# Two quads side by side through h's products on four PSUM banks, conversions doubled in other tiles of the first phase, the last product's three sums in tiles apart

## The chip, the core and the metric

One core of one Trainium2 chip. The metric is the device time of one execution in microseconds; the figures given are medians of several runs. The engines are PE (TensorE), DVE (VectorE), ACT (ScalarE), POOL (GpSimd) and SP, whose queue issues the transfers (DMA).

## What is computed

Three layers in a row on 4608 tokens, all in float32: attention within chunks of 64 tokens, then two feed-forward layers. The change is mostly in the last one, and a little in how the weights of the last two are converted.

```python
def _moe_ref(x, w_in, w_out, g_ln):          # 512 -> 1024 -> 512
    h = x @ w_in
    e = np.exp(h - np.max(h, axis=-1, keepdims=True))
    solu = h * (e / (np.sum(e, axis=-1, keepdims=True) + 1e-09))
    ...
    ln = (solu - mu) / np.sqrt(var + 1e-06) * g_ln
    return ln @ w_out

def _moe2_ref(x, w_in, w_out):               # 512 -> 2048 -> 512
    h = x @ w_in
    g = np.maximum(0.01 * h, h)
    return g @ w_out
```

The weights arrive as 64-bit words and are turned into float32 on the chip.

## The kernel before, in words

**First phase, 36 tiles of 128 tokens.** Loop t does attention, the first feed-forward layer and, beside them, the conversion of the weights of the last layer. A tile's order on PE is: half of ff1's products, transposes (pt), then for most tiles a block of 24 y matmuls (L499), then the x product (L389), which needs ACT's copy pt (L379), which stands behind the reduction z on DVE (L432) and the exponential on ACT (L434). In every fourth tile from t = 5 on (`late`: 5, 9, 13, ...) the y matmuls come at the tile's end, so they don't stand ahead of the x product. 40 pieces of weights are converted: normally one per tile, two in the tiles that the table `DOUBLE` names. A conversion is four instructions on DVE (L108, L110, L114, L118) and one on ACT. Every second piece completes a pair, and the pair step follows (`want_blocks`: DVE L191 and L192, five copies and subtractions on ACT and POOL) at the end of its tile.

**Last layer, six groups of 768 tokens.** Both products are done by seven products of half-size blocks instead of eight (the names p1 to p7, in the order `PRODUCTS`: p1, p6, p2, p7, p5, p4, p3). A float32 operand is split into a high and a low part (`operand`: ACT copies the high part, DVE subtracts it for the low one, L270 and L271), and each product is three matmuls: high by high, high by low, low by high.

*h's products* (the h stage, `h2_product`, L824): a quad is two blocks of 128 columns of the hidden layer, 8 quads per group. A quad has seven products of six matmuls of 384 columns; each product has weights of its own (`w_s`, a ring of 9 tiles, a load of 256 KB for each in the order of use, `w_order`). The products lie in three chains, each in one PSUM bank: p1 and p2 add up; p6, p7 and p4 add up; p5 and p3 add up. Between them a reader takes what is there so far: ACT copies p1 and takes p2 through the leaky function; DVE adds p1 to p6 (u2) and to p7 (u3), u3 to p5, p1 to p4, u2 to p3 (all L835), and ACT takes the last three through the leaky function (L806). There are two banks, `ptx` and `s`, and even and odd quads take them in opposite order. Two quads make a pair. After p5 of the odd quad the pair's first block is split for the next stage (`block_split`), in the next pair's first quad three sums of blocks are made on DVE (`block_sum`, L865).

*Output products* (`out_product`, `out_matmuls`, L883 and L901): 28 slots of 12 matmuls, seven products by four pairs. The sums of three tiles of 128 tokens lie in one PSUM tile of three banks, `o0` for the products 0, 2, 4, 6 and `o1` for 1, 3, 5, and `result` takes them out in adds over all three banks (L923). In the last group the last product is done one tile of tokens after the other, so that its results can leave in turn (L893 for the third).

Within each engine the order is the program's; an instruction behind a waiting one waits too.

## Time and profile before

| | |
|---|---|
| median of 3 runs (lowest to highest) | 1313.31 us (1312.67 to 1314.63) |
| profiled execution / its span | 1316.21 us / 1314.4 us |
| PE / weight loads / DVE / ACT / POOL busy | 96% / 84% / 67% / 43% / 21% of the span |
| mean granted clock of PE | 0.994 |
| first phase | up to 563.05 us |
| second group: h's products / output products | 687.17 to 752.03 / 752.03 to 811.37 us |
| a group, from start to start | 124.2 us |

PE is busy nearly all the time, so the time is to be looked for in what PE waits for and in the spacing of its matmuls; busy time of PE counts matmuls that overlap in its pipeline, and a matmul that is shown with 339 ns may follow the one ahead by half of that.

### The profile page before, as it was taken

The numbers are of one execution on the slowest core, as the hardware profiler recorded it, in microseconds if no ns is written. First come the engines' busy times: TensorE is split into PE (matmuls) and PEld (weight loads), VectorE is DVE, ScalarE is ACT, GpSimd is POOL, SyncE is SP. The second block draws the span as 40 slices with busy tenths as digits, with TensorE's granted clock in tenths as the row PEclk, the third lists the DMA queues.
The fourth block names the chain that finished last, engine by engine and source line by source line (L and its number), as shares of the span: only waits on it lengthen the run. The fifth ranks groups of instructions, "written<-read, shape, count | busy, mean of one in ns | idle before, by whom it ended". The sixth has DMA issues, their size and how long they took to land.

```text
span 1314.4 us, 21334 instructions
## 1 busy us (share of the span) xinstructions
PE 1259.7 (96%) x7978; PEld 1104.6 (84%) x7978; DVE 879.8 (67%) x1280; ACT 567.9 (43%) x1006; POOL 270.5 (21%) x356
## 2 busy tenths in 40 slices
PE   6999999999999999999999999999999999999998
PEld 4778887887888788898888989888889898889887
DVE  8777776777677675435784677567656765774574
ACT  6655444544554454423433352343334323443350
POOL 0346554564555464100000000000000000000000
PEclk9999999999999999999999999999999999999999
DMA  8534555666566564278888778878987898788575
GB/s 241 152 103 136 191 174 169 209 225 181 167 192 207 154 201 131 100 252 262 276 282 294 237 244 293 270 241 259 293 268 227 258 294 257 237 269 271 169 218 182
DMA packets 171638, 288.73 MB, mean 220 GB/s; under 512 B 50576, under 2 KB 81296, under 8 KB 170512
## 3 DMA queue, kind: packets, MB, share of 16 engines
q1 hardware_dynamic: 171152, 286.78, 69.6%
q8 instruction: 64, 1.05, 0.3%
q10 hardware_dynamic: 384, 0.59, 0.2%
q14 instruction: 38, 0.31, 0.1%
HBM read 239.08 MB, written 48.23 MB: 219 GB/s over the span
## 4 chain that ended last, share of the span: by engine, by line
PE 84%; DVE 6%; ACT 4%; issue 2%; POOL 1%; DMA 1%; ACTq 0%; SPq 0%; DVEq 0%; POOLq 0%
PE h_ps L824 25%; PE o_ps L883 18%; PE y_ps L499 13%; PE h_ps L417 11%; PE o_ps L901 9%; PE x_ps L389 3%; PE s_ps L340 2%; PE ln_ps L472 2%; DVE h_c L835 2%; DMA kbd<-in_k 1%; ACT yo L270 1%; PE pt_ps L373 1%; DVE lnT L487 1%; ACT c L806 1%; DVE es L353 1%
## 5 line engine op out<-in xcount | busy, mean ns | idle before, releaser
L824 PE MATMUL h_ps<-yo,w_s 128*128 128x384 f32 x2016 | 366.3, 339 | 23.9 <-DVE h_c L835 23.8
L824 PEld LDWEIGHTS h_ps<-yo,w_s 128*128 128x128 f32 x2016 | 349.5, 188 | 39.9 <-DVE h_c L835 35.8
L883 PE MATMUL o_ps<-wo_s,yo 128*128 128x512 f32 x1000 | 353.5, 397 | 0.0
L901 PE MATMUL o_ps<-wo_s,yo 128*128 128x256 f32 x1008 | 283.7, 281 | 0.0
L883 PEld LDWEIGHTS o_ps<-wo_s,yo 128*128 128x128 f32 x1000 | 187.7, 188 | 46.2
L417 PE MATMUL h_ps<-wi,xs 128*128 128x512 f32 x864 | 210.7, 397 | 2.6 <-ACT xs L403 1.4
L499 PE MATMUL y_ps<-lnT,wo 128*128 128x512 f32 (+1 forms) x888 | 205.2, 387 | 1.7 <-DVE lnT L487 0.9
L417 PEld LDWEIGHTS h_ps<-wi,xs 128*128 128x128 f32 x864 | 159.8, 189 | 38.3 <-ACT xs L403 2.7
L499 PEld LDWEIGHTS y_ps<-lnT,wo 128*128 128x128 f32 x888 | 161.4, 188 | 35.4 <-DVE lnT L487 2.0
L901 PEld LDWEIGHTS o_ps<-wo_s,yo 128*128 128x128 f32 x1008 | 190.0, 188 | 0.0
L271 DVE TENSOR_TENSOR yo<-c,yo 128x768 fp32r<-128x768 f32 x144 | 132.5, 952 | 31.9 <-ACT yo L270 31.9
L806 ACT ACTIVATE c<-h_c 128x384 f32<-128x384 f32 x144 | 74.2, 525 | 176.7 <-DVE h_c L835 174.7
L835 DVE TENSOR_TENSOR h_u<-h_ps,h_p 128x384 f32<-128x384 f32 x96 | 53.4, 556 | 124.6 <-PE h_ps L824 124.6
L270 ACT ACTIVATE yo<-c 128x768 fp32r<-128x768 f32 x144 | 113.1, 839 | 8.4 <-DVE c L865 6.8
L439 DVE SCALAR_TENSOR_TENSOR us<-h_ps,us 128x1024 f32<-128x1024 f32 x36 | 44.1, 1224 | 58.8 <-ACT us L434 58.8
L835 DVE TENSOR_TENSOR h_c<-h_ps,h_u 128x384 f32<-128x384 f32 x96 | 53.2, 554 | 33.4 <-PE h_ps L824 30.1
L487 DVE TENSOR_TENSOR lnT<-ln_ps,lnT 128x512 fp32r<-128x512 f32 x72 | 46.1, 683 | 33.6 <-ACT lnT L483 33.5
L363 POOL TENSOR_TENSOR es<-es,st 128x512 f32<-128x512 f32 x33 | 34.6, 1049 | 160.6 <-DVE st L362 151.1
L270 ACT ACTIVATE yo<-a 128x768 fp32r<-128x768 f32 x36 | 30.0, 842 | 72.8 <-DVE a L265 72.8
L389 PEld LDWEIGHTS x_ps<-pt,vbd 128*64 128x64 f32 x1152 | 39.1, 145 | 22.2 <-ACT pt L379 12.4
L507 ACT ACTIVATE ys<-y_ps 128x512 f32<-128x512 f32 x36 | 21.5, 597 | 83.1 <-PE y_ps L499 81.9
L806 ACT ACTIVATE c<-h_ps 128x384 f32<-128x384 f32 x48 | 23.6, 493 | 76.3 <-PE h_ps L824 76.3
(91 smaller groups left out, 1429.3 us busy)
## 6 DMA issues: line engine op xcount, KB each, us to landing
w_s<-wi_d SPq DMA_DIRECT2D x336, 256.0 KB, 3.4
wo_s<-wo_d SPq DMA_DIRECT2D x168, 512.0 KB, 4.5
wi_d<-wi SPq DMA_DIRECT2D x8, 1792.0 KB, 6.5
wo_d<-wi SPq DMA_DIRECT2D x8, 1792.0 KB, 6.8
raw<-in_w_out SPq DMA_DIRECT2D x24, 512.0 KB, 5.2
raw<-in_w_in SPq DMA_DIRECT2D x23, 512.0 KB, 5.3
vbd<-in_v SPq DMA_DIRECT2D x72, 128.0 KB, 4.6
a<-y_d SPq DMA_DIRECT2D x24, 384.0 KB, 4.4
```

The source lines that it names most:

```text
L270: act.activation(o[:, 0], x, AF.Copy)
L271: dve.tensor_tensor(o[:, 1], x, o[:, 0].bitcast(F32), op=ALU.subtract)
L389: pe.matmul(ps[e * D : (e + 1) * D, i, c * D : (c + 1) * D], lhsT=vv[:, i, c, e], rhs=pp[:, i, c * D : (c + 1) * D], start=True, stop=True,)
L417: pe.matmul(h[:, n, :], lhsT=x[:, a, kk, :], rhs=w[:, b, kk % 2, n, :], start=(kk == 0 and a == 0 and b == 0), stop=(kk == KD - 1 and a == 1),
L439: dve.scalar_tensor_tensor(u, h, 1.0 / FF1, u, op0=ALU.mult, op1=ALU.mult, accum_out=z[:, 2:3])
L487: dve.tensor_tensor(dst[:, 1], ps, dst[:, 0].bitcast(F32), op=ALU.subtract)
L499: pe.matmul(ps[:, part], lhsT=w[:, a, kk % 4, m * P : (m + 1) * P], rhs=lnT[:, c, kk, pairs, :][:, part], start=(kk == 0 and a == 0 and c ...
L806: act.activation(blocks[block, j // 2][:, j % 2], src, AF.Prelu, alpha=0.01)
L824: pe.matmul(ps, lhsT=w[:, a, kk * P : (kk + 1) * P], rhs=y[:, c, kk, :], start=(first and kk == 0 and a == 0 and c == 0), stop=(kk == 1 an ...
L835: dve.tensor_tensor(o, ps, x, op=ALU.add)
L883: pe.matmul(ps, lhsT=x[:, 0, kk, c], rhs=w[:, kk].rearrange("p a n -> p (a n)"), start=first, stop=False, skip_group_check=True,)
L901: pe.matmul(ps[:, : 2 * P], lhsT=x[:, 1, kk, c], rhs=w[:, kk, 0], start=False, stop=last, skip_group_check=True,)
```

## The change

Three edits.

1. The h stage takes two quads at a time: each product is done for both quads of a pair before the next product. The second quad's chains lie in two further banks, `b0` and `b1`. These are taken from the output sums: `o1` is now three tiles `b0`, `b1`, `b2` of a bank each, so its adds are done per bank. Loads, sums and splits are put at the corresponding places of the new order.
2. `DOUBLE` names other tiles: 10, 18 and 26 are out, 15, 23 and 31 are in.
3. In the last group the sums of the last product are three tiles of their own (`ptx`, `s`, and the third bank of `o`), and each result is taken out right behind its matmuls.

```diff
@@ -41,7 +41,7 @@
 RING = 11
 
 AHEAD = 5
-DOUBLE = (5, 6, 7, 10, 14, 18, 22, 26, 30)
+DOUBLE = (5, 6, 7, 14, 15, 22, 23, 30, 31)
 
 LN_SCALE = float(FF1) ** -3
 
@@ -277,7 +277,13 @@
             yo[g, PRODUCTS[k]] = operand(x)
 
     w_tiles = []
-    w_order = ((j, name) for _ in range(NG) for j in range(QUADS) for name in PRODUCTS)
+    w_order = (
+        (2 * u + i, name)
+        for _ in range(NG)
+        for u in range(PAIRS)
+        for name in PRODUCTS
+        for i in range(2)
+    )
 
     def w_load():
         at = next(w_order, None)
@@ -810,12 +816,15 @@
         def h2_product(n, k):
             g, j = divmod(n, QUADS)
             name = PRODUCTS[k]
-            even = n % 2 == 0
-            if k < 2:
-                banks[n, k] = bank(("ptx", "s")[k if even else 1 - k], "h2_ps")[:, :TH]
-            ps = banks[n, 0 if name in ("p1", "p2", "p5", "p3") else 1]
-            if k == 4:
-                ps = banks[n, 0] = bank(("ptx", "s")[0 if even else 1], "h2_ps")[:, :TH]
+            i, even = n % 2, n // 2 % 2 == 0
+            chain = 0 if name in ("p1", "p2", "p5", "p3") else 1
+            if name in ("p1", "p6", "p5"):
+                at = chain if even else 1 - chain
+                if i == 0:
+                    banks[n, chain] = bank(("ptx", "s")[at], "h2_ps")[:, :TH]
+                else:
+                    banks[n, chain] = pso.tile([P, 512], F32, tag=f"b{at}", name="h2_ps")[:, :TH]
+            ps = banks[n, chain]
             w, y = w_tiles.pop(0), yo[g, name]
             w_load()
             first, last = name in ("p1", "p6", "p5"), name in ("p2", "p4", "p3")
@@ -836,20 +845,20 @@
                 return o
 
             if name == "p1":
-                p = kept["p1"] = wb.tile([P, TH], F32, tag="h_p1", bufs=2, name="h_p1")
+                p = kept["p1", i] = wb.tile([P, TH], F32, tag="h_p1", bufs=2, name="h_p1")
                 act.activation(p, ps, AF.Copy)
             elif name == "p6":
-                kept["u2"] = with_ps("u2", kept["p1"])
+                kept["u2", i] = with_ps("u2", kept["p1", i])
             elif name == "p2":
                 leaky(n, "c11", ps)
             elif name == "p7":
-                kept["u3"] = with_ps("u3", kept["p1"])
+                kept["u3", i] = with_ps("u3", kept["p1", i])
             elif name == "p5":
-                leaky(n, "c22", with_ps("c", kept["u3"]))
+                leaky(n, "c22", with_ps("c", kept["u3", i]))
             elif name == "p4":
-                leaky(n, "c21", with_ps("c", kept["p1"]))
+                leaky(n, "c21", with_ps("c", kept["p1", i]))
             else:
-                leaky(n, "c12", with_ps("c", kept["u2"]))
+                leaky(n, "c12", with_ps("c", kept["u2", i]))
 
         def block_sum(name, i):
             x, y, op, to = {
@@ -875,7 +884,7 @@
 
         def out_matmuls(p, i, kk, m, whole=True):
             x, w = operands[p * PAIRS + i], wo_now[i]
-            ps = sums[p % 2][:, m]
+            ps = sums[p % 2][m]
             first = p in (0, 1, 4) and i == 0 and kk == 0
             last = i == PAIRS - 1 and kk == 1
             c = slice(m * P, (m + 1) * P)
@@ -909,10 +918,21 @@
 
         wo_now, results = {}, {}
 
-        def out_product(s):
+        def out_banks(p, apart):
+
+            if p == 1:
+                sums[1] = [pso.tile([P, 512], F32, tag=f"b{m}", name="o_ps") for m in range(3)]
+            else:
+                o = pso.tile([P, 3, 512], F32, tag="o", name="o_ps")
+                sums[0] = [o[:, m] for m in range(3)]
+                if apart:
+                    sums[0][:2] = [bank(tag, "o_ps") for tag in ("ptx", "s")]
+                sums["whole"] = None if apart else o
+
+        def out_product(s, apart):
             p, i = divmod(s, PAIRS)
             if i == 0 and p in (0, 1, 4):
-                sums[p % 2] = pso.tile([P, 3, 512], F32, tag=f"o{p % 2}", name="o_ps")
+                out_banks(p, apart and p == 4)
             wo_now[i] = wo_tiles.pop(0)
             wo_load()
             for kk in range(2):
@@ -920,7 +940,12 @@
                     out_matmuls(p, i, kk, m)
 
         def plus(o, p, a, x, m=slice(0, 3)):
-            dve.tensor_tensor(o[:, m], sums[p % 2][:, m, a * 2 * P : (a + 1) * 2 * P], x[:, m], op=ALU.add)
+            c = slice(a * 2 * P, (a + 1) * 2 * P)
+            if p % 2 == 0 and sums["whole"] is not None:
+                dve.tensor_tensor(o[:, m], sums["whole"][:, m, c], x[:, m], op=ALU.add)
+                return
+            for i in range(m.start, m.stop):
+                dve.tensor_tensor(o[:, i], sums[p % 2][i][:, c], x[:, i], op=ALU.add)
 
         def result(p, m=slice(0, 3), halves=(1, 0)):
 
@@ -940,7 +965,7 @@
             o = results[to]
             for a in halves:
                 if x is None:
-                    act.activation(o[:, m], sums[p % 2][:, m, 2 * P :], AF.Copy)
+                    act.activation(o[:, m], sums["whole"][:, m, 2 * P :], AF.Copy)
                 else:
                     plus(o, p, a, results[x], m)
                 x = to
@@ -957,28 +982,30 @@
             )
 
         for g in range(NG):
-            for j in range(QUADS):
-                if g == 0 and j < WOS:
-                    wo_load()
-                elif g and j == 1:
-                    out_store(g - 1, 6)
-                elif g and 2 <= j < 6:
-                    y_load(g + 1, j - 2)
-                for k in range(7):
-                    h2_product(g * QUADS + j, k)
-                    if g and j == 7 and k < 2:
-                        y_sum(g + 1, ("s1", "s3")[k])
-                    if j % 2 == 1 and k == 4:
-                        block_split(j // 2)
-                    if j % 2 == 0 and j and 1 <= k < 4:
-                        block_sum(("s1", "s3", "s2")[k - 1], j // 2 - 1)
+            for u in range(PAIRS):
+                for m in range(14):
+                    if m in (0, 7):
+                        if g == 0 and u < 3:
+                            wo_load()
+                        elif g and (u, m) == (0, 7):
+                            out_store(g - 1, 6)
+                        elif g and u in (1, 2):
+                            y_load(g + 1, 2 * u - 2 + m // 7)
+                    k, i = divmod(m, 2)
+                    h2_product(g * QUADS + 2 * u + i, k)
+                    if g and u == 3 and m in (0, 7):
+                        y_sum(g + 1, "s3" if m else "s1")
+                    if m == 8:
+                        block_split(u)
+                    if u and m in (2, 4, 6):
+                        block_sum(("s1", "s3", "s2")[m // 2 - 1], u - 1)
             for s in range(SLOTS):
                 p, i = divmod(s, PAIRS)
                 tail = g == NG - 1 and p == 6
                 if tail:
                     wo_now[i] = wo_tiles.pop(0)
                 else:
-                    out_product(s)
+                    out_product(s, g == NG - 1)
                 if s < 2:
                     for name in ("s1", "s3") if s == 0 else ("s2",):
                         block_sum(name, PAIRS - 1)
@@ -1007,9 +1034,9 @@
             for i in range(PAIRS):
                 for kk in range(2):
                     out_matmuls(6, i, kk, m, whole=m < 2)
-            if m:
-                result(6, slice(m - 1, m))
-                out_store(NG - 1, 6, sync, slice(m - 1, m))
+            if m < 2:
+                result(6, slice(m, m + 1))
+                out_store(NG - 1, 6, sync, slice(m, m + 1))
         result(6, slice(2, 3), (0,))
         for eng, rows in ((sync, slice(0, 64)), (act, slice(64, P))):
             out_store(NG - 1, 6, eng, slice(2, 3), rows)
```

On PE, at the end of the first pair and the start of the second (h2_ps are the banks' tiles, yo the operands in the order of the products, w_s the weights), before:

```order
L824 MATMUL h2_ps_5789<-yo_5510,w_s_5689 128x384 x6
L824 MATMUL h2_ps_5759<-yo_5513,w_s_5699 128x384 x6
L824 MATMUL h2_ps_5789<-yo_5516,w_s_5710 128x384 x6
L824 MATMUL h2_ps_5828<-yo_5493,w_s_5722 128x384 x6
L824 MATMUL h2_ps_5839<-yo_5500,w_s_5734 128x384 x6
L824 MATMUL h2_ps_5828<-yo_5504,w_s_5749 128x384 x6
```

and after:

```order
L833 MATMUL h2_ps_5752<-yo_5510,w_s_5392 128x384 x6
L833 MATMUL h2_ps_5768<-yo_5510,w_s_5668 128x384 x6
L833 MATMUL h2_ps_5689<-yo_5513,w_s_5679 128x384 x6
L833 MATMUL h2_ps_5700<-yo_5513,w_s_5690 128x384 x6
L833 MATMUL h2_ps_5752<-yo_5516,w_s_5701 128x384 x6
L833 MATMUL h2_ps_5768<-yo_5516,w_s_5711 128x384 x6
L833 MATMUL h2_ps_5828<-yo_5493,w_s_5721 128x384 x6
L833 MATMUL h2_ps_5839<-yo_5493,w_s_5730 128x384 x6
```

Before, these are p5, p4, p3 of the odd quad and p1, p6, p2 of the next one, each on the bank of the product two ahead; now each operand stands twice in a row and a bank comes back after four products.

DVE at the same place (h_u2, h_u3 and h_c are the adds, the yo row is the second half of the block's split, s1 a sum of blocks), before:

```order
L835 TENSOR_TENSOR h_u3_5787<-h2_ps_5759,h_p1_5757 128x384
L835 TENSOR_TENSOR h_c_5798<-h2_ps_5789,h_u3_5787 128x384
L271 TENSOR_TENSOR yo_5801<-c110_5697,yo_5801 128x768
L835 TENSOR_TENSOR h_c_5812<-h2_ps_5759,h_p1_5757 128x384
L835 TENSOR_TENSOR h_c_5823<-h2_ps_5789,h_u2_5768 128x384
L835 TENSOR_TENSOR h_u2_5848<-h2_ps_5839,h_p1_5837 128x384
L865 TENSOR_TENSOR s10_5850<-c210_5732,c220_5720 128x768
```

and after:

```order
L844 TENSOR_TENSOR h_u3_5750<-h2_ps_5700,h_p1_5687 128x384
L844 TENSOR_TENSOR h_c_5761<-h2_ps_5752,h_u3_5738 128x384
L271 TENSOR_TENSOR yo_5765<-c110_5719,yo_5765 128x768
L844 TENSOR_TENSOR h_c_5777<-h2_ps_5768,h_u3_5750 128x384
L844 TENSOR_TENSOR h_c_5788<-h2_ps_5689,h_p1_5676 128x384
L844 TENSOR_TENSOR h_c_5800<-h2_ps_5700,h_p1_5687 128x384
L844 TENSOR_TENSOR h_c_5811<-h2_ps_5752,h_u2_5698 128x384
L844 TENSOR_TENSOR h_c_5823<-h2_ps_5768,h_u2_5709 128x384
L844 TENSOR_TENSOR h_u2_5859<-h2_ps_5850,h_p1_5837 128x384
L874 TENSOR_TENSOR s10_5861<-c210_5790,c220_5763 128x768
```

The split stood between the odd quad's adds of p5 and p4; now it stands between the p5 adds of the first and the second quad, with five adds behind it until the next pair.

DVE in the first phase, from the end of t = 12 to the start of t = 13, before:

```order
L353 TENSOR_TENSOR es_2054<-s_ps_2036,st8_2052 128x512
L487 TENSOR_TENSOR lnT_449<-ln_ps_2057,lnT_449 128x4x128
L487 TENSOR_TENSOR lnT_449<-ln_ps_2062,lnT_449 128x4x128
L191 TENSOR_TENSOR wc_2083<-wf_1949,wc_2083 128x256
L192 TENSOR_TENSOR wc_2083<-wf_1809,wc_2083 128x256
L432 TENSOR_REDUCE z_2098<-h_ps_1951 128x1
L439 SCALAR_TENSOR_TENSOR us_2100,z_2098<-h_ps_1951,us_2100 128x1024
```

and after:

```order
L359 TENSOR_TENSOR es_2046<-s_ps_2028,st8_2044 128x512
L493 TENSOR_TENSOR lnT_449<-ln_ps_2049,lnT_449 128x4x128
L493 TENSOR_TENSOR lnT_449<-ln_ps_2054,lnT_449 128x4x128
L438 TENSOR_REDUCE z_2077<-h_ps_1943 128x1
L445 SCALAR_TENSOR_TENSOR us_2079,z_2077<-h_ps_1943,us_2079 128x1024
```

The pair step (the two wc rows) stood ahead of the reduction z of t = 13; now it is at the end of t = 11 and of t = 13.

DVE at t = 15, between the softmax's reciprocal and x's split, before:

```order
L362 RECIPROCAL st8_2503<-st8_2503 128x8
L108 TENSOR_SCALAR wf_2553<-wf_2553 128x512
L110 TENSOR_SCALAR wf_2553<-wf_2553 128x512
L114 SCALAR_TENSOR_TENSOR wf_2553<-raw_2131,wf_2553 128x512
L118 SCALAR_TENSOR_TENSOR wf_2553<-raw_2131,wf_2553 128x512
L407 TENSOR_TENSOR xs_2652<-x_ps_2622,xs_2652 128x512
```

and after:

```order
L368 RECIPROCAL st8_2343<-st8_2343 128x8
L108 TENSOR_SCALAR wf_2393<-wf_2393 128x512
L108 TENSOR_SCALAR wf_2395<-wf_2395 128x512
L110 TENSOR_SCALAR wf_2393<-wf_2393 128x512
L110 TENSOR_SCALAR wf_2395<-wf_2395 128x512
L114 SCALAR_TENSOR_TENSOR wf_2393<-raw_1970,wf_2393 128x512
L114 SCALAR_TENSOR_TENSOR wf_2395<-raw_2110,wf_2395 128x512
L118 SCALAR_TENSOR_TENSOR wf_2393<-raw_1970,wf_2393 128x512
L118 SCALAR_TENSOR_TENSOR wf_2395<-raw_2110,wf_2395 128x512
L413 TENSOR_TENSOR xs_2500<-x_ps_2470,xs_2500 128x512
```

One conversion, now two; the same holds for t = 23 and 31, and t = 10, 18 and 26 have one instead of two.

PE in the last product of the last group, from the second to the third tile of tokens (with the engines that a row waits for), before:

```order
L901 MATMUL o_ps_12449<-wo_s_12538,yo_12582 128x256
L883 MATMUL o_ps_12449<-wo_s_12538,yo_12582 128x512
L901 MATMUL o_ps_12449<-wo_s_12538,yo_12582 128x256
L893 MATMUL o_ps_12449<-wo_s_12484,yo_12535 128x256 [waits DVE_49]
L893 MATMUL o_ps_12449<-wo_s_12484,yo_12535 128x256
L901 MATMUL o_ps_12449<-wo_s_12484,yo_12535 128x256
```

and after:

```order
L910 MATMUL o_ps_12531<-wo_s_12624,yo_12668 128x256
L892 MATMUL o_ps_12531<-wo_s_12624,yo_12668 128x512
L910 MATMUL o_ps_12531<-wo_s_12624,yo_12668 128x256
L902 MATMUL o_ps_12529<-wo_s_12566,yo_12621 128x256 x2
L910 MATMUL o_ps_12529<-wo_s_12566,yo_12621 128x256
L902 MATMUL o_ps_12529<-wo_s_12566,yo_12621 128x256 x2
```

The third part wrote into the same tile as the second and waited for DVE; now it has a tile of its own and no wait at that place.

## Rows read from the trace of the kernel before

**Rows 1.** The page, costliest groups: busy us, mean ns | idle before, releaser

```profile
L824 PE MATMUL h_ps<-yo,w_s 128*128 128x384 f32 x2016 | 366.3, 339 | 23.9 <-DVE h_c L835 23.8
```

**Rows 2.** Timeline of PE, 683 to 760: start, us, what [idle before <-releaser]

```profile
687.17 14.83 PE L824 MATMUL h_ps<-yo,w_s 128*128 128x384 f32 x84
703.32 15.43 PE L824 MATMUL h_ps<-yo,w_s 128*128 128x384 f32 x84 [1.32 <-DVE h_c L835]
...
752.03 0.39 PE L883 MATMUL o_ps<-wo_s,yo 128*128 128x512 f32 x1
```

**Rows 3.** The chain of waits in order of time, 686 to 722: start, us, what

```profile
687.33 12.59 PE h_ps L824 x72
```

**Rows 4.** Timeline of all engines, 700 to 722, end of an odd quad

```profile
716.70 0.56 DVE L835 TENSOR_TENSOR h_c<-h_ps,h_u 128x384 f32<-128x384 f32 x1 [0.48 <-PE h_ps L824]
...
718.58 0.96 DVE L271 TENSOR_TENSOR yo<-c,yo 128x768 fp32r<-128x768 f32 x1 [1.33 <-ACT yo L270]
...
719.46 0.55 DVE L835 TENSOR_TENSOR h_c<-h_ps,h_p 128x384 f32<-128x384 f32 x1
```

**Rows 5.** Windows: length, busy PE, PEld, DVE, ACT, POOL (count), PEclk, DMA, GB/s

```profile
201.50:203.20 1.70, 1.70 (x19) 1.37 (x15) 1.63 (x3) 0.72 (x3) 1.53 (x4) 0.50 0.97 405
564.00:574.00 10.00, 10.00 (x59) 10.00 (x58) 3.35 (x6) 3.24 (x7) 0.00 (x0) 1.00 0.87 283
687.00:703.00 16.00, 15.00 (x86) 14.63 (x85) 7.54 (x12) 4.69 (x9) 0.00 (x0) 1.00 0.94 314
703.00:712.00 9.00, 8.68 (x47) 8.15 (x48) 5.97 (x10) 3.03 (x6) 0.00 (x0) 1.00 0.81 252
752.00:811.50 59.50, 59.50 (x339) 51.70 (x338) 46.38 (x53) 25.78 (x35) 0.00 (x0) 1.00 0.82 257
```

**Rows 6.** DMA over one h stage, 687.17 to 752.03

```profile
DMA packets 9839, 17.34 MB, mean 267 GB/s; under 512 B 979, under 2 KB 2771, under 8 KB 9835
```

**Rows 7.** Timeline of PE, first phase, tiles 9, 13 and 17

```profile
138.18 0.60 PE L373 MATMUL pt_ps<-ident,es 128*128 128x128 f32 x4
...
152.80 0.60 PE L373 MATMUL pt_ps<-ident,es 128*128 128x128 f32 x4
...
195.96 0.60 PE L373 MATMUL pt_ps<-ident,es 128*128 128x128 f32 x4
...
199.67 1.89 PE L389 MATMUL x_ps<-pt,vbd 128*64 128x64 f32 x32 [2.24 <-ACT pt L379]
...
214.28 0.60 PE L373 MATMUL pt_ps<-ident,es 128*128 128x128 f32 x4
...
258.89 1.15 PE L389 MATMUL x_ps<-pt,vbd 128*64 128x64 f32 x32
```

**Rows 8.** Timeline of DVE and ACT there: z, a double, a single conversion, pt

```profile
196.11 1.21 DVE L432 TENSOR_REDUCE z<-h_ps 128x1 f32<-128x1024 f32 x1
...
215.64 1.59 DVE L108 TENSOR_SCALAR wf<-wf 128x512 f32<-128x512 f32 x2
...
219.03 1.28 DVE L118 SCALAR_TENSOR_TENSOR wf<-raw,wf 128x512 uint32<-128x512 uint32 x2
...
233.48 0.38 DVE L108 TENSOR_SCALAR wf<-wf 128x512 f32<-128x512 f32 x1
...
236.52 0.69 DVE L407 TENSOR_TENSOR xs<-x_ps,xs 128x512 fp32r<-128x512 f32 x1
...
255.32 1.21 DVE L432 TENSOR_REDUCE z<-h_ps 128x1 f32<-128x1024 f32 x1
...
258.24 0.59 ACT L379 ACTIVATE pt<-pt_ps 128x512 f32<-128x512 f32 x1
```

**Rows 9.** Timeline of the last 9 us

```profile
1305.77 0.88 DVE L923 TENSOR_TENSOR o_u<-o_ps,o_u 128x256 f32<-128x256 f32 x2 [3.70 <-PE o_ps L901]
...
1306.70 0.50 PE L893 MATMUL o_ps<-wo_s,yo 128*128 128x256 f32 x2 [0.98 <-DVE o_u L923]
...
1309.84 1.22 DVE L923 TENSOR_TENSOR o_u<-o_ps,o_u 128x256 f32<-128x256 f32 x3 [3.19 <-PE o_ps L901]
```

## The prediction, as it was made before the result

> **What bounds the kernel now.** I read the page first: the group of h's products, L824, is the only one of PE's large groups with idle time ahead of it, 23.9 us, nearly all put down to one add of DVE, h_c [rows 1]. So I looked at PE alone in one of the six groups of 768 tokens. The stretch of h's products (the h stage) runs from 687.17 to 752.03, 64.86 us, in four runs of 84 matmuls with a hole of 1.32 us ahead of each but the first [rows 2]; the other five groups show the same four runs and the same three holes. What would it take with no wait? The chain of waits gives it: at a group's start 72 matmuls follow one another in 12.59 us with nothing between them, 174.9 ns each or 1.049 us per product of six [rows 3]. 336 of them make 58.77 us. The h stage is therefore 6.09 us over its own pace: 3 x 1.32 = 3.96 us in the holes and 2.1 us in waits too short to show as holes.
>
> Why the hole? At the end of the odd quad DVE does p5's add at 716.70. Then comes the split's second half (yo), which waits 1.33 us for ACT, and only behind it p4's add, over at 719.46 + 0.55 = 720.01 [rows 4]. That add frees the bank in which the next quad begins. From p5's add to a free bank are 3.31 us. PE has two products to do meanwhile, 2 x 1.049 less the 0.16 us by which a matmul's 339 ns stick out over the pace [rows 1, 3], 1.93 us. The difference, 1.38 us, is the hole of 1.32 within 0.06, so this arithmetic can be used for the change.
>
> Is 174.9 ns a floor? In 564 to 574 the weight loads are busy 10.00 of 10.00 us at full clock [rows 5]: matmul behind matmul, each with weights of its own. And can the weights come faster? The stage moved 17.34 MB [rows 6]; at the 314 GB/s of its first 16 us [rows 5] that takes 55.2 us, less than 58.77.
>
> **The change, part by part.**
>
> *Two quads side by side.* The number of matmuls and adds stays. Between a product and the next use of its bank there are now three others instead of one. The tightest place is p3 of the second quad: it needs p5's add of that quad, which stands behind the split on DVE, in the place where p4's add stood. From the end of the first quad's p5, PE does p5, p4, p4, p3: 4 x 1.049 - 0.16 = 4.03 us, against 3.31 + 0.05 for the add. 0.67 us are left. The next pair's first products take the banks of p4 and p3, whose adds follow on DVE at 0.55 us each [rows 4] or as soon as their product is done, and which PE wants only one by one, 1.05 us apart. The sums that now stand between u2's and u3's adds are followed by three products. In the last pair of four groups an extra sum goes ahead of p5's add; it eats the 0.67 us at most about once per group, which I take as nothing. The first group's second product takes a bank that the first phase's last copies read: once, and one product's 1.05 us at most; also nothing. Taken: all 6.09 us go, 6 x 6.09 = 36.5 us. Ends: 6 x 3.96 = 23.8 us if only the holes go, 36.5 us.
>
> *Order of the weight loads, sums and stores.* The same number of equal loads in the order of use; the store and the loads of y on SP's queue stay ahead of the same products (7, 14, 21, 28, 35), and the block's split stands behind the first quad's p5, three products after the p2 that completes the block. Nothing.
>
> *Conversions doubled in other tiles.* In the first phase every fourth tile (t = 5, 9, 13, ...) is one in which PE has no y matmuls ahead of the x product. At t = 13, 21 and 29 PE waits there for ACT's copy pt, 2.24 us at 199.67 [rows 7]. DVE's pair step (L191, L192) of the tile before stood ahead of the reduction z, which began at 196.11, only after the tile's transposes of 195.96. The x product begins 3.56 us after z there, and 3.57 us at t = 17 (258.89 after 255.32), where no pair step stood ahead and PE didn't wait [rows 7, 8]: z sets it. The tile t = 13 takes 214.28 - 195.96 = 18.32 us, t = 9 takes 152.80 - 138.18 = 14.62 [rows 7]: 3.70 us, of which 1.46 are PE at half clock after the hole (0.50 at 201.5 [rows 5]). In the new table no late tile has a pair step ahead: 3 x 3.70 = 11.1 us gained.
>
> But t = 14 and 15 are both doubled (so are 22, 23 and 30, 31). A single conversion keeps DVE from 233.48 to 236.52, 3.04 us, and is over exactly when x's split is ready; a double one takes from 215.64 to 219.03 + 1.28 = 220.31, 4.67 us [rows 8]. t = 14 has slack, as a tile after a late one. t = 15 has none, since DVE enters it just as late as it now enters with a single one. So DVE leaves t = 15 1.63 us later, and t = 16 has no idle time in which to win that back. At t = 16 PE's y matmuls still cover it; at t = 17 nothing does: the copy pt, at 258.24 + 0.59 only 0.06 us ahead of the x product at 258.89 [rows 7, 8], comes 1.57 us too late. New holes of 1.57 us at t = 17, 25 and 33: 4.7 us. Does the clock fall after them? After 1.32 us it doesn't (1.00 in 703 to 712, right behind such a hole), after 2.24 it does [rows 5, 7]; 1.57 is nearer the former, so I take no fall. With a fall it is 3 x 1.46 = 4.4 us more. Net gain 11.1 - 4.7 = 6.4 us; ends 2.0 and 11.1.
>
> *Adds in three parts.* The second sum now lies in three tiles, so three sums per group are added in 18 adds of 256 instead of 6 of 768. An add of 256 takes 0.44 us [rows 9], all 18 take 7.9 us. Even as pure addition, DVE would be busy 46.38 + 7.9 = 54.3 of the 59.5 us of an output stage, in which PE is busy throughout [rows 5]; each sum has at least four slots of products before its banks are wanted. Nothing. A rule speaks against it: by the Trainium skill ("VectorE: DVE Perf Modes", section "The TRN2 errata") an instruction pays a fixed extra, once for a large tile and each time for many small ones. The trace agrees: 384 elements take 0.55 us and 256 take 0.44 [rows 4, 9], so some 0.2 us don't depend on the size. If those of the 12 further adds per group lay on the path, 6 x 12 x 0.2 = 14 us, the sum below would be 30 us instead of 45; they lie under PE's products.
>
> *The tail.* Now the sums of the last product share a tile: PE waits 0.98 us for the add of part two before it may write part three, and the last add is the third of three that follow 1309.84 (1.22 us) [rows 9]. With tiles apart PE ends 0.98 us sooner and one add of 0.44 is left of 1.22: 0.98 + 0.78 = 1.8 us. Ends 0.8 and 2.0.
>
> **The sum.** 36.5 + 6.4 + 1.8 = 44.7 us. The profiled execution took 1316.2 us (span 1314.4): 1271.5. The median of the runs is 2.9 us lower, so 1313.3 - 44.7 = 1268.6 us.
>
> **Rivals.**
> - *The clock falls after the new holes* too: 1268.6 + 4.4 = 1273.0. The hole lies between the two lengths seen. 0.22.
> - *No new holes*, because DVE finds the 1.63 us somewhere: 1263.9. Against it: no idle row of DVE in t = 15 and 16 but those in which it waits for ACT in its own chain. 0.15.
> - *DMA sets the h stage.* A faster PE asks for more at once. If 283 GB/s (564 to 574) is what the weights get at best, the stage takes 17.34 MB / 283 = 61.3 us and gives only 3.6 us per group: 1283.7. Against: 314 GB/s in [rows 5]. 0.08.
> - *The holes move instead of going.* If DVE's chain for two quads is 1.32 us longer than I make it, p3 of each pair waits 0.65 us, 24 x 0.65 = 15.6 us: 1284.2. 0.06.
> - *Slower:* the 252 GB/s of 703 to 712, where y loads run beside the weights, are a ceiling and not merely what was asked for. Then the h stage takes 17.34 / 252 = 68.8 us, 3.9 longer than now, and 6 x 3.9 - 6.4 - 1.8 gives 1328.7. It decides below 262 GB/s (66.2 us, which uses up the other gains). Against: a DMA share of 0.81 there and 0.94 in 687 to 703. 0.03, and 0.01 for landing on no change.
> - *A lower floor:* if the 174.9 ns still hold waits too short to see, and PE streams a column per cycle of its 2.4 GHz (a granted clock of 1.00), 384 columns take 160 ns, and 14.9 ns x 2016 = 30 us more go: 1238.6. Against: the stretch without waits has weight loads busy throughout [rows 3, 5]. 0.03. The Trainium skill ("TensorE: Matmul & The Clock Gate", section "Back-to-back issue gap") gives columns / 2.4 + 2.5 ns, 162.5 ns here, by which the sum would be 25 us larger; this trace is 12.4 ns above it.
>
> **How the numbers follow.** The forecast has the rest, 0.42. With the two cases beside it, 1263.9 to 1273.0 hold 0.79; unknown small waits in the h stage and the two cases at 1284 pull the upper end: 1262 to 1284. Within 0.2% (2.6 us, about what a measurement of this kernel tells from no change) 0.01, slower 0.04, faster 0.95.
>
> **What would show it.** After: h stages of 58.8 us without holes at L833 (61 would speak for DMA, with waits for w_s loads; holes at p3 with h_c as releaser for DVE); no hole before x at t = 13, 21, 29 and holes of about 1.6 us at t = 17, 25, 33, with a granted clock of 1.00 or 0.50 behind them; no wait ahead of L902 and the last add alone. Wrong would be above all an h stage that keeps its 64.9 us.

## The result and the profile after

| | before | after |
|---|---|---|
| median (lowest to highest) | 1313.38 us (1312.67 to 1314.63) | 1266.2 us (1265.91 to 1266.87) |
| profiled execution / its span | 1316.21 / 1314.4 us | 1266.87 / 1265.1 us |
| PE / weight loads / DVE / ACT busy | 96 / 84 / 67 / 43% | 98 / 87 / 69 / 45% |
| first matmul of h's products | 563.05 us | 555.29 us |
| h stage of the second group | 64.86 us | 58.35 us |

The ratio is 0.9641, 95% interval 0.9624 to 0.9657: 47.2 us less, where 44.7 were forecast (1268.6 us, range 1262 to 1284).

The costliest groups on the page of the kernel after, with the DMA issues for h's weights (busy time, mean ns | idle time ahead, releaser; for the issue KB and us to landing):

```profile
PE 1238.4 (98%) x7978; PEld 1098.8 (87%) x7978; DVE 874.8 (69%) x1356; ACT 566.0 (45%) x1006; POOL 269.6 (21%) x356
...
L833 PE MATMUL h_ps<-yo,w_s 128*128 128x384 f32 x2016 | 350.9, 334 | 0.0
L833 PEld LDWEIGHTS h_ps<-yo,w_s 128*128 128x128 f32 x2016 | 349.1, 188 | 0.9
...
w_s<-wi_d SPq DMA_DIRECT2D x336, 256.0 KB, 4.0
```

h's products (L824 before, L833 now) had 23.9 us of idle time ahead of them [rows 1] and have none; DVE makes more instructions (1356 instead of 1280, the adds in three parts) in less busy time, and PE waits for none of the adds of the last layer.

PE alone in the second group, kernel after (start, duration, what ran; a number in brackets would be a hole ahead of the row):

```profile
672.92 58.50 PE L833 MATMUL h_ps<-yo,w_s 128*128 128x384 f32 x336
731.27 0.39 PE L892 MATMUL o_ps<-wo_s,yo 128*128 128x512 f32 x1
```

One row holds the whole stage, where before there were four with a hole ahead of three [rows 2]. From start to start it is 731.27 - 672.92 = 58.35 us, 173.7 ns per matmul; the other five groups read 58.24 to 58.37. Busy time by stretch (PE first, weight loads second; granted clock, DMA share and GB/s at the end) shows that nothing is left between the matmuls:

```profile
673.10:731.70 58.60, 58.60 (x339) 58.42 (x339) 35.30 (x56) 21.57 (x42) 0.00 (x0) 1.00 0.91 298
```

Weight loads fill 58.42 of 58.60 us at full clock, beside 298 GB/s. That the loads set the pace isn't shown by this. The y matmuls of the first phase have 512 columns and weights of their own too:

```profile
520.11 11.07 PE L505 MATMUL y_ps<-lnT,wo 128*128 128x512 f32 x48
531.02 1.91 PE L478 MATMUL ln_ps<-ident,us 128*128 128x128 f32 x16
```

From start to start they take 10.91 / 48 = 227.3 ns each, with loads of the same size busy for only 8.87 of 10.80 us (520.2 to 531) and a granted clock of 1.00. 128 further columns cost 53.6 ns, 0.42 ns a column, which is one column per cycle of 2.4 GHz; and both paces lie about 14 ns above that (160 and 213.3 ns). So by these two widths the pace is made by the columns and some fixed 14 ns per matmul, an estimate; where the 14 ns come from stays open. The 252 and 283 GB/s of [rows 5] were what was asked for, no ceiling.

PE in the first phase, kernel after: the holes at t = 17 and 25, and the s product behind the first of them.

```profile
256.08 1.15 PE L395 MATMUL x_ps<-pt,vbd 128*64 128x64 f32 x32 [1.25 <-ACT pt L385]
257.06 1.05 PE L346 MATMUL s_ps<-kbd,qt 128*64 128x128 f32 x16
...
372.91 1.15 PE L395 MATMUL x_ps<-pt,vbd 128*64 128x64 f32 x32 [1.25 <-ACT pt L385]
```

The 2.24 us of t = 13 [rows 7] and its like at 21 and 29 are gone, and 1.25 us stand at t = 17, 25 and 33 (at 489.79) where 1.57 were expected. The x product behind them takes 1.15 us, its length at full clock (1.89 behind the old hole at 199.67 [rows 7]).

### The profile page after: what moved, and what is told of

The parts are those of the page before. It is cut to its first block, busy times and chain, and to the rows that moved or that the text cites. A ratio compares the mean times of both kernels' runs of the same rounds, so it can differ in the third digit from the quotient of the medians.

```text
span 1265.1 us, 21471 instructions
## 1 busy us (share of the span) xinstructions
PE 1238.4 (98%) x7978; PEld 1098.8 (87%) x7978; DVE 874.8 (69%) x1356; ACT 566.0 (45%) x1006; POOL 269.6 (21%) x356
## 3 DMA queue, kind: packets, MB, share of 16 engines
q8 instruction: 64, 1.05, 0.3%
## 4 chain that ended last, share of the span: by engine, by line
PE 91%; DVE 4%; ACT 2%; DMA 1%; issue 1%; POOL 0%; SPq 0%; ACTq 0%
PE h_ps L833 28%; PE o_ps L892 19%; PE y_ps L505 14%; PE h_ps L423 13%; PE o_ps L910 9%; PE x_ps L395 3%; PE s_ps L346 2%; PE ln_ps L478 2%; PE pt_ps L379 1%; DMA raw<-in_w_in 1%; DVE lnT L493 1%; DVE wf L114 0%; ACT es L576 0%; DVE es L359 0%; DMA qt<-in_q 0%
## 5 line engine op out<-in xcount | busy, mean ns | idle before, releaser
L833 PE MATMUL h_ps<-yo,w_s 128*128 128x384 f32 x2016 | 350.9, 334 | 0.0
L833 PEld LDWEIGHTS h_ps<-yo,w_s 128*128 128x128 f32 x2016 | 349.1, 188 | 0.9
L445 DVE SCALAR_TENSOR_TENSOR us<-h_ps,us 128x1024 f32<-128x1024 f32 x36 | 44.1, 1225 | 50.8 <-ACT us L440 50.8
L440 ACT ACTIVATE us<-h_ps,z 128x1024 f32<-128x1024 f32 x36 | 40.1, 1115 | 43.0 <-DVE z L438 42.9
L362 ACT ACTIVATE es<-es 128x512 f32<-128x512 f32 x33 | 20.9, 632 | 84.8 <-DVE es L359 84.4
```

The source lines that it names most:

```text
L440: act.activation(u, h, AF.Exp, bias=z[:, 0:1], accum_out=z[:, 1:2])
L445: dve.scalar_tensor_tensor(u, h, 1.0 / FF1, u, op0=ALU.mult, op1=ALU.mult, accum_out=z[:, 2:3])
L833: pe.matmul(ps, lhsT=w[:, a, kk * P : (kk + 1) * P], rhs=y[:, c, kk, :], start=(first and kk == 0 and a == 0 and c == 0), stop=(kk == 1 an ...
```

## Experiments

**The three edits one by one, and the adds in three parts.** First edit alone (the kernel after with two edits taken back):

```diff
-DOUBLE = (5, 6, 7, 14, 15, 22, 23, 30, 31)
+DOUBLE = (5, 6, 7, 10, 14, 18, 22, 26, 30)
...
-                    out_product(s, g == NG - 1)
+                    out_product(s, False)
...
-            if m < 2:
-                result(6, slice(m, m + 1))
+            if m:
+                result(6, slice(m - 1, m))
```

> The first edit alone: two quads side by side on four banks (with the second sum in three tiles, which it needs); the conversions are doubled in the tiles of before and the last product's sums share a tile as before. Theory: the three edits act in stages apart, so their gains add up. The h stage goes from 64.86 to 58.35 us (the trace of after), 6 x 6.5 = 39.0 us, so 1313.3 - 39.0 = 1274.3 us; the three holes of the first phase (2.24 us at t = 13, 21, 29) and the waits of the tail (0.98 us) stand as before. The forecast's own size for it was 36.5 us, 1276.8. Rival: a faster h stage takes back part of what the first phase gains (or hands it on), for instance because the h stage of the first group starts with fewer weights loaded; then this run is not 1274.3 but nearer 1266.2 or 1280, and the three runs do not add up to the 47.2 us of the whole.

Measured: 1274.31 us (ratio 0.9696, 0.9682 to 0.9709), 39.3 us below the 1313.64 of the kernel before beside it. The h stage of its second group is one row of 58.50 us for 336 matmuls, as after.

Second edit alone (the kernel before with the new table):

```diff
-DOUBLE = (5, 6, 7, 10, 14, 18, 22, 26, 30)
+DOUBLE = (5, 6, 7, 14, 15, 22, 23, 30, 31)
```

> The second edit alone: the kernel before with the conversions doubled in the tiles 14 and 15, 22 and 23, 30 and 31. Theory: the first h matmul comes 7.76 us earlier (563.05 to 555.29, as in the two traces) and the rest is unchanged, 1313.3 - 7.8 = 1305.5 us, with holes of 1.25 us at t = 17, 25 and 33 and none at 13, 21 and 29. The forecast's size for it was 6.4 us, 1306.9. Rival: the gain in the first phase came from something else in the changed kernel (the order of the first loads of the last layer, PSUM tiles), and the table alone gives less than 6 us, over 1307.3.

Measured: 1307.79 us, 5.9 us less (ratio 0.9952, 0.9940 to 0.9965: 4.6 to 7.9 us). The holes are those of the kernel after (1.26 to 1.27 us at t = 17, 25 and 33), and h's first matmul stands at 554.81 us in this profile (563.05 before, 555.29 after): the table alone makes the holes and the whole gain of the first phase, which refutes the rival. But the gain lies below the 7.8 us between the two profiled executions and, by the median, just under the 6 us at which the rival was drawn, with the interval on both sides of it. Why a difference of two profiles overstates the gain is seen in the clock. PE in this run at the hole of t = 5, which no edit touches:

```profile
72.21 1.15 PE L389 MATMUL x_ps<-pt,vbd 128*64 128x64 f32 x32 [2.29 <-ACT pt L379]
73.19 1.04 PE L340 MATMUL s_ps<-kbd,qt 128*64 128x128 f32 x16
```

and in the kernel before:

```profile
72.77 1.39 PE L389 MATMUL x_ps<-pt,vbd 128*64 128x64 f32 x32 [2.30 <-ACT pt L379]
73.94 1.93 PE L340 MATMUL s_ps<-kbd,qt 128*64 128x128 f32 x16
```

The same hole, and once the s product (the next on PE) takes 1.04 us, once 1.93. In the 13 profiles that stand in this document there are 25 holes of 2.23 to 2.31 us in the first phase: 17 have slow matmuls behind them, 8 have none. The profiled execution of before has four of four; it lay 2.8 us above its median.

Third edit alone (the kernel before; `o1` stays one tile):

```diff
+                if apart:
+                    sums[0][:2] = [bank(tag, "o_ps") for tag in ("ptx", "s")]
...
-            if m:
-                result(6, slice(m - 1, m))
+            if m < 2:
+                result(6, slice(m, m + 1))
```

> The third edit alone: the kernel before, with the three sums of the last product of the last group in tiles apart; the second sum stays in one tile of three banks. Theory: PE no longer waits 0.98 us ahead of the last part and one add of 0.44 us instead of three is left after it: 1.8 us by the forecast, 2.2 us by the traces of before and after, 1311.1 to 1311.5 us. Rival: the last store sets the end anyway and only the 0.98 us go, 1312.3 us.

Measured: 1311.52 us, 2.1 us less (ratio 0.9978, 0.9968 to 0.9989). DVE at its end:

```profile
1303.85 0.88 DVE L941 TENSOR_TENSOR o_u<-o_ps,o_u 128x256 f32<-128x256 f32 x2 [1.94 <-PE o_ps L901]
1306.69 0.42 DVE L941 TENSOR_TENSOR o_u<-o_ps,o_u 128x256 f32<-128x256 f32 x1 [1.95 <-PE o_ps L901]
```

The last part's single add waits for PE, and nothing else is left behind PE, where before three adds followed [rows 9]. The rival (only 0.98 us) would be 1312.7 beside 1313.64; the interval, 1309.4 to 1312.2, leaves it out.

The second sum in three tiles, alone (the kernel before):

```diff
-                sums[p % 2] = pso.tile([P, 3, 512], F32, tag=f"o{p % 2}", name="o_ps")
+                sums[1] = [pso.tile([P, 512], F32, tag=f"b{m}", name="o_ps") for m in range(3)]
...
+            for i in range(m.start, m.stop):
+                dve.tensor_tensor(o[:, i], sums[p % 2][i][:, c], x[:, i], op=ALU.add)
```

> The kernel before, with the second sum of the output products in three tiles of a bank each, so that three sums per group are taken out in 18 adds of 256 columns instead of 6 of 768; quads, conversions and tail as before. Theory: 12 further adds per group with some 0.2 us of fixed cost each (2.4 us per group on DVE) lie under PE's products: 1313.3 us, within 1 us. Rival (by the fixed cost on the path): 6 x 12 x 0.2 = 14 us slower, 1327.7 us; or half of it where the adds hold up the splits behind them on DVE, 1320.

Measured: 1314.32 us, ratio 1.0006 (0.9997 to 1.0014): no difference that can be told from noise (0.4 us less to 1.8 us more). The page of this run:

```profile
L883 PE MATMUL o_ps<-wo_s,yo 128*128 128x512 f32 x1000 | 353.5, 397 | 0.0
L901 PE MATMUL o_ps<-wo_s,yo 128*128 128x256 f32 x1008 | 283.7, 281 | 0.0
```

PE has no idle time in these two groups of output products although DVE makes 12 further adds per group. The parts add up by their medians: 39.3 + 5.9 + 2.1 = 47.3 us, against 47.2 for the whole. That this fits to 0.1 us is luck: each part is known to 1.4 to 1.8 us, and by the ratios the sum is 39.9 + 6.3 + 2.9 = 49.1. Within that the edits act apart.

**Where do the new holes come from?** If DVE enters t = 16 late because two doubled tiles follow one another, it must help to put the work where DVE has idle time, in t = 14 (and 22, 30). The kernel after with another table:

```diff
-DOUBLE = (5, 6, 7, 14, 15, 22, 23, 30, 31)
+DOUBLE, TRIPLE = (5, 6, 7), (14, 22, 30)
...
-                pieces = 0 if t in (1, 4) or t >= T - 2 else 2 if t in DOUBLE else 1
+                pieces = 0 if t in (1, 4) or t >= T - 2 else 2 if t in DOUBLE else 3 if t in TRIPLE else 1
```

The unchanged kernel after was measured beside it on the same chip:

> The changed kernel as it is, beside the runs below on the same chip: 1266.2 us, and against the kernel before a ratio of 0.964. In three profiles of kernels with the old holes the clock fell behind a hole of 2.2 to 2.3 us in some places and not in others; the one such hole left here (t = 5) may therefore show 1.00 or 0.50 behind it, worth about 1 us.

Measured: 1266.41 us (ratio 0.9649, 0.9635 to 0.9663), with no fall of the clock behind its hole at t = 5.

> The changed kernel with three conversions in the tiles 14, 22 and 30 and one in 15, 23 and 31, instead of two and two. Theory: the holes of 1.25 us at t = 17, 25 and 33 come from DVE, which leaves the second doubled tile late and has no idle time in t = 16 to win it back; t = 14 (and 22, 30), which stands behind a tile without y matmuls ahead of x, has 4.6 us of idle time on DVE (2.75 and 1.84 us in the trace), enough for two more conversions of 1.63 us each. So the three holes go, and with the one at t = 33 the wait of 0.75 us for lnT: 3.8 to 4.5 us, 1261.7 to 1262.4 us. Rival: the idle time isn't usable (it lies in waits of DVE's own chain), DVE enters t = 15 about as late as it now enters t = 16, and the hole stands at t = 15, 16 or 17 with 1 to 2 us: 1266 to 1269 us.

Measured: **1262.58 us** (1261.88 to 1263.72; ratio 0.9620, 0.9606 to 0.9635), 3.8 us below the kernel after. DVE in t = 14 of this run:

```profile
210.07 1.23 DVE L445 SCALAR_TENSOR_TENSOR us<-h_ps,us 128x1024 f32<-128x1024 f32 x1 [2.83 <-ACT us L440]
...
212.27 1.90 DVE L108 TENSOR_SCALAR wf<-wf 128x512 f32<-128x512 f32 x3
...
216.90 1.88 DVE L118 SCALAR_TENSOR_TENSOR wf<-raw,wf 128x512 uint32<-128x512 uint32 x3
218.75 0.69 DVE L413 TENSOR_TENSOR xs<-x_ps,xs 128x512 fp32r<-128x512 f32 x1
```

The three conversions keep DVE from 212.27 to 218.75, 6.48 us. That is 1.84 us more than the two of the kernel after take (211.57 to 216.21), and it goes into idle time that the kernel after has in this tile ahead of xs:

```profile
218.04 0.69 DVE L413 TENSOR_TENSOR xs<-x_ps,xs 128x512 fp32r<-128x512 f32 x1 [1.84 <-ACT xs L409]
```

So the tile still ends in time. Of the 4.6 us of idle time that were counted only this part was used; the wait of 2.83 us at L445 stands ahead of the conversions and remains. Between t = 13 and t = 33 PE has one hole left in this run:

```profile
491.55 5.75 PE L505 MATMUL y_ps<-lnT,wo 128*128 128x512 f32 x24 [0.73 <-DVE lnT L493]
```

All three holes ahead of x are gone, so the lag of DVE was their cause. The 0.75 us for lnT at t = 33 stayed as 0.73: the part of the expectation that counted it in was wrong.

**How much slack has the pair?** One, and in a second kernel three (`range(3)`), reductions without a reader ahead of p5's add of the second quad, in the kernel after:

```diff
                     if m == 8:
                         block_split(u)
+                        for _ in range(1):
+                            d = wb.tile([P, 1], F32, tag="h_d", name="h_d")
+                            dve.reduce_max(d, kept["u3", 0], axis=AX)
```

> The changed kernel with one further reduction over 384 columns on DVE (its result is used by nobody) in each of the 24 pairs of quads, behind the split of the block, so ahead of p5's add of the second quad. By rows of that size it takes about 0.5 us. Theory: p3 of the second quad has 0.67 us of slack by the forecast, 0.69 by the trace of after (the add is over 3.32 us after p5's end of the first quad, PE wants the bank 4.01 us after it); the reduction fits, and the time is 1266.2 us, within 1. Rival: the slack is used up already in waits too short to be seen; then each pair pays 0.5 us, 24 x 0.5 = 12 us, 1278 us.

> The same with three such reductions, about 1.5 us. Theory: 1.5 - 0.69 = 0.8 us per pair is left over, a hole at p3 of the second quad with DVE's h_c as releaser, 24 x 0.8 = 19 us: 1285 us. Rival with no slack: 24 x 1.5 = 36 us, 1302 us. Rival with more slack than worked out (another add sets the bank): under 1275 us.

Measured: 1269.01 us (ratio 0.9669, 0.9654 to 0.9683) and 1296.89 us (0.9880, 0.9864 to 0.9897), 2.6 and 30.5 us above the kernel after. PE in a group with one reduction:

```profile
673.13 57.39 PE L833 MATMUL h_ps<-yo,w_s 128*128 128x384 f32 x330
730.81 1.32 PE L833 MATMUL h_ps<-yo,w_s 128*128 128x384 f32 x6 [0.29 <-DVE h_c L844]
```

and with three:

```profile
692.42 14.84 PE L833 MATMUL h_ps<-yo,w_s 128*128 128x384 f32 x84 [0.88 <-DVE h_c L844]
708.13 14.86 PE L833 MATMUL h_ps<-yo,w_s 128*128 128x384 f32 x84 [0.88 <-DVE h_c L844]
723.87 14.85 PE L833 MATMUL h_ps<-yo,w_s 128*128 128x384 f32 x84 [0.88 <-DVE h_c L844]
740.17 1.32 PE L833 MATMUL h_ps<-yo,w_s 128*128 128x384 f32 x6 [1.46 <-DVE h_c L844]
741.33 0.39 PE L892 MATMUL o_ps<-wo_s,yo 128*128 128x512 f32 x1
```

One reduction moves the next add by 0.46 us (685.46 to 685.92) and fits in three of four pairs; in the last pair, where an extra sum stands ahead too, a hole appears. So there is slack, and the rival of 1278 us falls; the last pairs of four groups have it (0.28 to 0.29 us each), and their stages take 58.83 to 58.87 us instead of 58.35: 2.0 of the 2.6 us. The first and the last group, without that sum, show 336 matmuls in one row. Three move the add by 1.64 us and a pair then takes 708.13 to 723.87, 15.74 us instead of 14.59 (84 x 173.7 ns): 1.15 us more. **A hole of 0.88 us in the rows costs 1.15 us**: matmuls that run one into the other stand 0.16 us out over the pace, so the next one begins 0.88 + 0.16 = 1.04 us late, and by the starts of its matmuls the product behind the hole takes 1.15 to 1.17 us instead of 1.04. The slack is what the add could move before PE came late, 1.64 - 1.04 = 0.60 us, where the forecast had 0.67. My 1285 us was too low because of what a hole costs beyond its row and because the last pair pays 1.46.

**Does the clock fall behind a hole of 1.57 us?** Additions without a reader ahead of z make the three new holes longer; a second kernel has the sizes the other way round (5, 3, 1):

```diff
+                if t in (17, 25, 33):
+                    c = {17: 1, 25: 3, 33: 5}[t]
+                    d = wk.tile([P, 5, P], F32, tag="dd", bufs=1, name="dd")[:, :c]
+                    x = ident.unsqueeze(1).to_broadcast([P, c, P])
+                    dve.tensor_tensor(d, x, x, op=ALU.add)
                 if 1 <= t <= T:
                     solu_a(t - 1)
```

> The changed kernel with one further addition on DVE (its result is used by nobody) ahead of the reduction z in the tiles 17, 25 and 33, of 128, 384 and 640 columns, by rows of such sizes about 0.25, 0.5 and 0.85 us. The holes ahead of the x product there grow from 1.25 to about 1.5, 1.75 and 2.1 us. Without a fall of the clock the time is 1266.4 + 1.6 = 1268.0 us and the x product behind each hole takes 1.15 us and the s product 1.05. Rival, the fall that the forecast gave a chance of 0.22: behind the holes above 1.57 us at least the clock is 0.50 and each such place costs 1.46 us more, up to 1272.4 us. In the profiles so far no hole of 1.22 to 1.32 us had a fall behind it, and those of 2.2 to 2.3 us had one in some places and none in others.

> The same with the sizes the other way round, 640, 384 and 128 columns in the tiles 17, 25 and 33. If the length of the hole decides whether the clock falls, the tiles with and without a fall change places against the other run (17 and 33); if the place or the moment decides, they stay or differ without order. Time 1268.0 us without a fall, up to 1272.4 with three.

Measured: 1268.92 us (ratio 0.9663, 0.9647 to 0.9679) and 1268.29 us (0.9657, 0.9641 to 0.9673). PE in the first of them:

```profile
256.03 1.15 PE L395 MATMUL x_ps<-pt,vbd 128*64 128x64 f32 x32 [1.45 <-ACT pt L385]
...
373.32 1.15 PE L395 MATMUL x_ps<-pt,vbd 128*64 128x64 f32 x32 [1.72 <-ACT pt L385]
...
490.88 1.15 PE L395 MATMUL x_ps<-pt,vbd 128*64 128x64 f32 x32 [1.98 <-ACT pt L385]
491.96 4.58 PE L423 MATMUL h_ps<-wi,xs 128*128 128x512 f32 x12
```

and in the second, with the sizes changed over:

```profile
256.63 1.81 PE L395 MATMUL x_ps<-pt,vbd 128*64 128x64 f32 x32 [1.99 <-ACT pt L385]
258.22 1.93 PE L346 MATMUL s_ps<-kbd,qt 128*64 128x128 f32 x16
...
375.36 1.15 PE L395 MATMUL x_ps<-pt,vbd 128*64 128x64 f32 x32 [1.72 <-ACT pt L385]
...
492.39 1.15 PE L395 MATMUL x_ps<-pt,vbd 128*64 128x64 f32 x32 [1.46 <-ACT pt L385]
```

In these two profiles the fall moved with the longest hole: behind 1.45, 1.46 and twice 1.72 us the matmuls run at full speed, behind 1.98 and 1.99 they don't. 3.02 us of ff1 take 4.58 us in the first kernel (granted clock 0.62 in that stretch), and 1.05 us of s take 1.93 in the second (0.54 from 256.6 to 260). The forecast's 1.57 us lies between lengths behind which none of these tiles had a fall. But the length doesn't decide alone. The four executions of the second kernel took 1269.46 (the profiled one), 1269.41, 1267.18 and 1267.12 us, the first two at a mean granted clock of 0.996 and the others at 0.999: 2.3 us are about what a fall at t = 5 (0.8) and one at t = 17 (1.5) cost, so the other two probably had neither; they left no trace. And in the first 40 us, where one hole follows another, the clock fell behind a shorter one too: in the run with three conversions it is 0.53 from 32.4 to 36.0 us, right behind a hole of 1.15 us.

**How much lead do the weights need?** The kernel after with a shorter ring of weight tiles:

```diff
-WS = 9
+WS = 6
```

> The changed kernel with a ring of 6 instead of 9 tiles for the weights of h's products. The load for a tile is issued when the product that used it is over, 5 instead of 8 products ahead of its use. Theory: 5 x 1.042 = 5.2 us are more than the 4.0 us from issue to landing, so nothing waits: 1266.4 us within 1. Rival: the loads of y and the stores of results that share the queues make single loads late, which 8 products of lead covered and 5 do not: waits for w_s at L833, 1268 us and more; if DMA as a whole set the pace, it would be the same with 9, so this run cannot be faster.

Measured: 1286.6 us (ratio 0.9792, 0.9772 to 0.9813), 20 us above the kernel after; the rival was right, by far more than its 1268. The page's group for h's products and its issues, this run:

```profile
L833 PE MATMUL h_ps<-yo,w_s 128*128 128x384 f32 x2016 | 358.4, 336 | 12.1 <-DMA w_s<-wi_d 11.3 <-DVE h_c L844 0.4
...
w_s<-wi_d SPq DMA_DIRECT2D x336, 256.0 KB, 3.8
```

and PE in its third group:

```profile
795.45 6.41 PE L833 MATMUL h_ps<-yo,w_s 128*128 128x384 f32 x36
804.62 16.38 PE L833 MATMUL h_ps<-yo,w_s 128*128 128x384 f32 x84 [2.76 <-DMA w_s<-wi_d]
821.53 14.83 PE L833 MATMUL h_ps<-yo,w_s 128*128 128x384 f32 x84 [0.53 <-DMA w_s<-wi_d]
837.18 23.25 PE L833 MATMUL h_ps<-yo,w_s 128*128 128x384 f32 x132 [0.82 <-DMA w_s<-wi_d]
```

In all groups but the first, PE stops right behind the six products whose weights the ring holds at the stage's start. DMA issues of this run in the 13 us around that place (793 to 806; KB each, median us to landing), and the stretch 799 to 802:

```profile
w_s<-wi_d SPq DMA_DIRECT2D x6, 256.0 KB, 6.9
wo_s<-wo_d SPq DMA_DIRECT2D x2, 512.0 KB, 5.7
out<-o_p SPq DMA_DIRECT2D x1, 384.0 KB, 7.8
```

```profile
799.00:802.00 3.00, 2.86 (x17) 2.54 (x15) 0.96 (x2) 0.60 (x2) 0.00 (x0) 1.00 1.04 372
```

There the weights share the DMA engines, which are full at 372 GB/s, with the last loads for the output products and a store of results: 6.9 us to landing against 5.2 us of lead. Whether a load loses the time on the engines or behind others in SP's queue, this run doesn't tell. The six h stages are together 19.6 us longer than those of the kernel after, of which the rows show 11.3 as waits for w_s. I had taken the median over all issues, 4.0 us (3.8 on the page of this run), which says nothing of the start of a stage. Eight products of lead, 8.3 us, cover it.

## Why the prediction was right, step by step

- *Two quads side by side: 36.5 forecast, 39.3 measured alone.* The holes and the short waits went, as said. The mis-sized term is the stage's own pace: 174.9 ns was 12.59 / 72 [rows 3], and that stretch still held short waits. By the starts of its matmuls three of its twelve products took 1.07 us and the others 1.04, which makes up the difference. The stage runs at 173.7 ns, 58.35 instead of 58.77 us: 6 x 0.42 = 2.5 us, nearly the whole miss of the total. The slack that decided between this and the rival of moved holes (1284.2) was forecast as 0.67 us, and the two runs with reductions bear it out: 0.46 us fit in, and by three reductions it is 0.60. That DVE's adds held PE up is shown by the same run, in which later adds bring the holes back. That each operand now stands twice in a row gains nothing by itself: a product without a wait takes 1.04 us before and after.
- *Conversions doubled elsewhere: 6.4 forecast, 5.9 measured alone, by two errors that nearly cancel.* The lag was put at 1.63 us and gave a hole of 1.25, not 1.57: in the trace after, xs of t = 15 comes 3.31 us after the start of the x product instead of 1.86, so the lag was 1.45, and 1.29 of it were left at z of t = 17 (7.55 us after the x product of t = 16 instead of 6.26). The rows of after for it, DVE and then PE:

```profile
233.90 0.68 DVE L413 TENSOR_TENSOR xs<-x_ps,xs 128x512 fp32r<-128x512 f32 x1
...
252.53 1.22 DVE L438 TENSOR_REDUCE z<-h_ps 128x1 f32<-128x1024 f32 x1
```

```profile
230.59 1.15 PE L395 MATMUL x_ps<-pt,vbd 128*64 128x64 f32 x32
244.98 1.15 PE L395 MATMUL x_ps<-pt,vbd 128*64 128x64 f32 x32
```

and the two x products of before (its xs and z are in [rows 8]):

```profile
234.66 1.15 PE L389 MATMUL x_ps<-pt,vbd 128*64 128x64 f32 x32
...
249.06 1.15 PE L389 MATMUL x_ps<-pt,vbd 128*64 128x64 f32 x32
```

  The doubled conversion takes 4.56 us up to the start of the next row (229.34 to 233.90). The forecast's 4.67 ran to the end of its last row, which overlaps the next one, and was set against 3.04 taken from start to start. DVE also entered it 0.07 us earlier, and in t = 16 the single conversion takes 2.95 us (245.19 to 248.14) instead of 3.09 before (247.82 to 250.91): DVE won a little back, where I took nothing. Three holes shorter by 0.32 us are 1 us more than forecast. Against it, I took a clock fall of 1.46 us off all three old holes in the median too. In the four profiles with these holes at t = 13, 21 and 29, nine of twelve had a fall behind them, so about 1.1 us of the 4.4 weren't there to be won in a mean execution. By the same rows the shorter holes alone give 3 x (2.24 - 1.25) = 3.0 us; the other half of the gain is falls that no longer come, and it differs from one execution to the next.
- *No fall behind the new holes* (1273.0 otherwise): right, at 1.25 us. At the 1.57 us that were forecast no hole was measured; 1.46 and 1.72 had none.
- *Adds in three parts: nothing.* Right, 0.06% slower with an interval that holds zero and ends at 1.8 us. The 14 us by the fixed cost of a small instruction lay under PE's products.
- *The tail: 1.8 forecast, 2.1 measured alone* by the medians (2.9 by the ratio, 1.4 to 4.2).
- *DMA as the bound* (1283.7 and 1328.7): wrong, 298 GB/s over a whole stage and 372 in a full stretch. But the lead of the loads has less to spare than the median landing suggests, as the run with six tiles shows.
- *A lower floor* (160 ns): not seen. With every hole gone the pace is 173.7 ns at a granted clock of 1.00. The forecast's reason, weight loads busy throughout, doesn't hold: the rows of 512 columns have the same distance from a column per cycle with loads busy in 82% of the time. The estimate of 162.5 ns by the formula of the Trainium skill ("TensorE: Matmul & The Clock Gate", section "Back-to-back issue gap") isn't reached either. The Trainium skill calls the formula there the gap of an isolated matmul and says that it over-counts for a stream at 512 columns. This trace doesn't agree: it lies 11 ns above the formula at 384 columns and at 512 too (227.3 against 215.8 ns).

## What to carry to other kernels

Count, for each PSUM bank, the products that PE has to do between one use and the next, and hold that against the chain of readers behind which the bank's own reader stands; two independent blocks interleaved on twice the banks turned 1.3 us short into 0.6 us spare. On an engine that works in order, a doubled piece of work costs nothing only in a tile with idle time behind that work: two in a row handed their lag on until it met a place without cover, three at once in the idle tile didn't. The pace of a stretch is taken from start to start, and the price of a hole from the growth of the period, not from the hole's row.
